# Weights decoded in chunks of two slices, and a key load moved ahead of a store, in a kernel of banded attention and an MLP

## The chip, the cores and the metric

The program runs on one core of one Trainium2 chip. The metric is the device time of one execution in microseconds (us). TensorE does the matmuls, VectorE, ScalarE and GpSimd the elementwise work, and SyncE issues nearly all DMAs. In the profile they are called PE (PEld for the weight loads), DVE, ACT, POOL and SP.

## The reference

```python
B, H, S, D = 4, 8, 768, 64          # n_global = 8, n_local = 96
def _attn_ref(q, k, v, n_global, n_local):
    scores = np.matmul(q, k.transpose(0, 1, 3, 2)) / np.sqrt(D)
    rel = pos[:, None] - pos[None, :]
    is_global = pos[None, :] < n_global
    is_local = (rel >= 0) & (rel < n_local)
    dist = np.where(is_global & ~is_local, n_local, np.abs(rel))
    scores = np.where(is_global | is_local, scores - slopes * dist, -1e9)
    a = np.exp(scores - scores.max(-1, keepdims=True))
    return np.matmul(a / (a.sum(-1, keepdims=True) + 1e-9), v)

def _moe_ref(x, w_in, w_out):       # x: 3072 x 512, w_in: 512 x 2048, w_out: 2048 x 512
    h = x @ w_in
    return (h * np.clip(h + 3.0, 0.0, 6.0) / 6.0) @ w_out
```

The attention's output, heads side by side, is x. The weights `w_in` and `w_out` come as 64-bit floats, q, k and v as 32-bit floats.

## The kernel before

**Blocks and pairs.** The 3072 rows are cut into 8 blocks of 384. A block is first attended, in 4 pairs of heads (32 pairs in all, numbered through), and then goes through the MLP. A pair has three tiles of 128 rows, t = 0, 1, 2. Its scores are matmuls (`scores`, L857 or L861), `weigh` adds the distances and finds the row maximum on DVE (L872) and takes the exponential on ACT (L876), `sum_up` forms the reciprocals on DVE, and `normalize` multiplies on POOL (L896). From block 2 on `spread(t)` transposes 32x32 blocks on DVE (L921) and stores them through SP to a scratch in DRAM (`there`, L923). `fetch` brings a pair's three tiles back as `weights` with four DMAs (L930), and `values` (L948) multiplies by v. `put_x` splits the result into a high and a low part, `xh` on ACT and `xl` on DVE.

**The MLP.** The inner 2048 are cut into 16 slices, numbered f. A step of a slice is `first(f)`, 12 matmuls into `hp` (L175), `gate` (ACT L186, then DVE L187, giving `g`), a high part `gh` (ACT L195, or POOL L193 from block 2 on), the rest `gl` (DVE L200), and `second(f)`, 9 matmuls (L207) into three accumulators. `second` of a slice follows `first` of the next one. Each product is formed from high and low parts, three matmuls for one.

**The decode.** The 64-bit weights are turned on the chip into a high and a low 32-bit part. The host lays them out in 32 chunks of 512 KB, one slice of `w_in` and one of `w_out` in turn. A chunk is fetched by SP (`wst`, L372), and takes these passes over 128x512 words: a magnitude on ACT (`wz`, L380), a scaled low word on POOL (`we`, L384), a clamp and a shift on DVE (L411, L412), the sign on ACT (into `we`, L391), an addition on DVE (L421), the high part on ACT (`w1h` or `w2h`, L425), and the low part on DVE (`w1l` or `w2l`, L418). There are three buffers of `wst` and two each of `wz` and `we`. The generator `decode` gives out the work in three steps a chunk, each with a DVE price; `work` calls it as long as the DVE price given out is below the PE time given out, and `decoded_to` forces what a slice needs.

**Stages.** While the first 8 pairs (blocks 0 and 1) are attended, the decode begins. Then block 0's 16 steps run with the decode beside them and 4 of block 1's steps among them. The remaining 12 steps of block 1 run beside block 2's attention (`beside`): a list of units, one unit per half step, into which a pair's parts are placed, 4 units per pair; `scale` (L840, giving `qs`) prepares a pair's queries on ACT. From there on each block's MLP runs beside the next block's attention.

**Order.** PE, SP and POOL run in the order in which the program is written (`in_order`). DVE's and ACT's order is set by a list scheduler, from that order and its own timing. Every engine, and SP's queue of DMA issues too, executes in order: an instruction that waits holds what is behind it. Keys and queries of a pair are loaded by `load_next(n, False)` into the place of pair n, for pair n + 2, once pair n's scores are done. Values are loaded by `load_next(n, True)`.

The general path (`general`, `weight_chunk`) is compiled and not executed for these sizes.

Of the kernel before, what the change touches and what calls it, by code (L numbers as in the profile page):

```python
# [10 lines left out]
F32R = mybir.dt.float32r  # L11
I32 = mybir.dt.int32
U32 = mybir.dt.uint32
I16 = mybir.dt.int16
F16 = mybir.dt.float16
AF = mybir.ActivationFunctionType
ALU = mybir.AluOpType
# [33 lines left out]
WAKE = 9  # L51
BESIDE = 12
LEAST_AHEAD = 4
WORDS = 3
DOWN = 2.0 ** -95

def store(nc, pool, out, row, acc, last=False):
# [6 lines left out]
class Kernel:  # L64
# [15 lines left out]
    def decoding(self, ctx, loads, bufs, **kw):  # L80

        self.wp = self.pool("wp", loads, ctx=ctx, **kw)
        self.zp = self.pool("zp", bufs, ctx=ctx, **kw)
        self.ep = self.pool("ep", bufs, ctx=ctx, **kw)

    def weights(self):

# [33 lines left out]
    def weight_chunk(self, i):  # L121

        nc = self.nc
        f = i // 2
        if i % 2 == 0:  # L130
            hi, lo = self.w1(self.w1h, f), self.w1(self.w1l, f)
            sh = lambda a: a.rearrange("p (k c) -> p k c", k=NKT)
        else:
            hi, lo = self.w2(self.w2h, f), self.w2(self.w2l, f)
            sh = lambda a: a
        st = self.wp.tile([P, 2 * DM], I32, name="wst")
        z = self.zp.tile([P, DM], I32, name="wz")
        e = self.ep.tile([P, DM], I32, name="we")
        nc.sync.dma_start(out=st, in_=self.w[i])
# [12 lines left out]
        nc.vector.tensor_tensor(out=lo, in0=sh(zf), in1=hi.bitcast(F32), op=ALU.subtract)  # L152
# [215 lines left out]


    def fetch(self, i):  # L370
        self.raw[i] = self.wp.tile([P, 2 * DM], I32, name="wst")
        self.nc.sync.dma_start(out=self.raw[i], in_=self.w[i])  # L372

    def magnitude(self, i):


        words = self.raw[i].rearrange("p (c w) -> p c w", w=2)
        self.z[i] = self.zp.tile([P, DM], I32, name="wz")
        self.e[i] = self.ep.tile([P, DM], I32, name="we")
        self.nc.scalar.activation(out=self.z[i].bitcast(F32), in_=words[:, :, 1].bitcast(F32), func=AF.Abs, scale=DOWN)  # L380
# [3 lines left out]
        self.nc.gpsimd.tensor_scalar(out=self.e[i], in0=words[:, :, 0].bitcast(U32), scalar1=2.0 ** -29, scalar2=0.0, op0=ALU.mult, op1=ALU.add)  # L384

    def signs(self, i):


        top = self.raw[i].bitcast(I16).rearrange("p (c w) -> p c w", w=4)[:, :, 3]
        over = self.e[i].bitcast(F16).rearrange("p (c w) -> p c w", w=2)[:, :, 1]  # L390
        self.nc.scalar.activation(out=over, in_=top, func=AF.Sign, scale=-1.0, bias=self.half)  # L391

    def part(self, i, w1, w2):
        f = i // 2
        return (self.w1(w1, f), lambda a: a.rearrange("p (k c) -> p k c", k=NKT)) if i % 2 == 0 else (self.w2(w2, f), lambda a: a)

    def decode(self):

        nc = self.nc
        ts, tt = nc.vector.tensor_scalar, nc.vector.tensor_tensor
        N = 2 * NF
        self.magnitude(0)
        for i in range(N + 1):
            a, b = i < N, i > 0
            if a:
                if i + 2 < N:
                    self.fetch(i + 2)
                z = self.z[i]  # L410
                ts(out=z.bitcast(F32), in0=z.bitcast(F32), scalar1=LEAST * DOWN, scalar2=MOST * DOWN, op0=ALU.max, op1=ALU.min)  # L411
                ts(out=z, in0=z, scalar1=3, scalar2=None, op0=ALU.logical_shift_left)  # L412
                self.signs(i)
            yield 0.78 * a
            if b:
                hi, sh = self.part(i - 1, self.w1h, self.w2h)
                lo, _ = self.part(i - 1, self.w1l, self.w2l)
                tt(out=lo, in0=sh(self.z.pop(i - 1).bitcast(F32)), in1=hi.bitcast(F32), op=ALU.subtract)  # L418
            yield 0.64 * b
            if a:  # L420
                tt(out=z, in0=z, in1=self.e.pop(i), op=ALU.add)  # L421
# [3 lines left out]
                nc.scalar.copy(out=hi, in_=sh(z.bitcast(F32)))  # L425
            yield 0.66 * a

    def work(self, pe, dve):

# [5 lines left out]
    def decode_step(self):  # L435
        self.given[1] += next(self.decoding_steps)
        self.decoded += 1
        if self.decoded == 3 * (2 * NF + 1):
            self.decoded_all()

    def decoded_to(self, i):

        while self.decoded < 3 * (i + 1) + (2 if i < 2 * NF - 1 else 3):
            self.decode_step()

    def halves(self, steps, pool=False):


        for block, f, x, acc in steps:
            self.decoded_to(2 * f)  # L450
# [30 lines left out]

    def finish(self):
        block, f, acc, gh, gl = self.last
        self.decoded_to(2 * f + 1)
# [8 lines left out]
    def banded(self, flag):  # L493
# [12 lines left out]
        with ExitStack() as early, ExitStack() as words:  # L506
            x0 = self.x_tiles(self.pool("x0", 1, ctx=early, side="right"))
            xs = [x0, self.x_tiles(), self.x_tiles()]
            self.decoding(words, WORDS, 2, side="right")
            self.decoding_steps = self.decode()  # L510

            def decoded_all():
# [3 lines left out]
            self.decoded_all = decoded_all  # L516
            self.fetch(0)
            self.given[1] = LEAD
            self.allowed = 3 * NF + 2
# [57 lines left out]
            self.allowed = 3 * (2 * NF + 1)  # L577
# [46 lines left out]
    def beside(self, x):  # L624
# [4 lines left out]
        pairs[0].scale()  # L629
        for p, me in enumerate(pairs):  # L630
            at = units[4 * p + 2:]
            weigh = lambda t, me=me: me.scores(t)()
            even = lambda t, me=me: (me.sum_up(t), me.normalize(t))
            at[0] += [lambda weigh=weigh: weigh(0), lambda weigh=weigh: weigh(1)]
            at[1] += [lambda even=even: even(0), lambda even=even: even(1)]
            if p + 1 < NPAIR:
                at[1].append(pairs[p + 1].scale)
            at[2] += [lambda weigh=weigh: weigh(2), lambda me=me: me.spread(0), lambda me=me: me.spread(1)]
            at[3] += [lambda even=even: even(2), lambda me=me: me.spread(2)]
            at[4] += [me.fetch, lambda me=me: self.load_next(me.n, False)]  # L640
# [43 lines left out]
    def general_setup(self):  # L684
# [2 lines left out]
        self.common(1, 2)  # L687
        self.weights()
        self.weights()
        self.decoding(self.ctx, 1, 1)  # L690
        self.ap_ = self.pool("ap", 1)
        self.dp = self.pool("dp", 1)
        self.up = self.pool("up", 1)
# [335 lines left out]
```

## Time and profile before

| | us |
|---|---|
| median of 3 runs | 684.6 |
| their range | 681.65 to 684.73 |
| the profiled execution | 682.72 |
| its span, first to last instruction | 680.9 |

1.8 us lie around the span. PE is busy for 655.4 us of it (96%), DVE for 416.2 (61%), ACT for 297.6 (44%), POOL for 213.4 (31%). The chain of work that ended last is made of PE for 78%. Since matmuls overlap, busy time of PE is not a rate; the number of matmuls in a stretch tells more. In the rows below, a row of the stages has the stretch, its length, then busy us and (x instructions) of PE, PEld, DVE, ACT and POOL, the granted clock of PE, the busy share of the DMA engines and GB/s. A row of a group has line, engine, operation, out<-in, shape and count, then busy us, mean ns of one, and the engine's idle time before them with what ended it.

### The profile page before, as it was taken

What the parts mean: (1) busy time and instruction counts of PE and PEld (TensorE: products, weight loads), DVE (VectorE), ACT (ScalarE), POOL (GpSimd) and SP (SyncE); (2) the same over time, 40 slices, a digit from 0 to 9 for tenths busy, and PEclk for the clock granted to TensorE, in tenths of its full rate; (3) what the DMA queues carried; (4) which work ended last, traced back from release to release, by engine and by line L of the source; (5) the groups of instructions that cost most, each with busy time, mean ns of one, the idle gap of its engine ahead of it and who ended that gap; (6) DMA issues with size and microseconds to landing.
All of it is one profiled execution on the core that took longest, in us unless ns stands there. A gap on an engine that the chain in (4) does not pass through costs nothing.

```text
span 680.9 us, 11393 instructions
## 1 busy us (share of the span) xinstructions
PE 655.4 (96%) x3923; PEld 580.3 (85%) x3923; DVE 416.2 (61%) x1132; ACT 297.6 (44%) x762; POOL 213.4 (31%) x389
## 2 busy tenths in 40 slices
PE   9878999999897999999999999999999999999997
PEld 7767888887676999899999999999998999988995
DVE  6887999935354776557762777547763677422222
ACT  6897888844343443143331444143331434221111
POOL 5661222202111333315440444404541344302110
PEclk9999899999899999999999999999999999999999
DMA  8565555213655357634554256634465155500001
GB/s 292 153 228 167 189 185 183 97 48 82 169 143 152 104 149 198 163 124 118 151 155 135 83 152 185 180 113 116 124 163 155 66 156 143 139 32 17 1 1 52
DMA packets 69476, 89.58 MB, mean 132 GB/s; under 512 B 10912, under 2 KB 54176, under 8 KB 69408
## 3 DMA queue, kind: packets, MB, share of 16 engines
q1 hardware_dynamic: 69120, 88.49, 44.6%
q8 instruction: 33, 0.54, 0.3%
q14 instruction: 35, 0.29, 0.1%
q10 hardware_dynamic: 288, 0.26, 0.1%
HBM read 65.14 MB, written 23.59 MB: 130 GB/s over the span
## 4 chain that ended last, share of the span: by engine, by line
PE 78%; DVE 6%; DMA 6%; ACT 4%; issue 2%; POOL 2%; SPq 1%; DVEq 0%; POOLq 0%; ACTq 0%
PE hp L175 34%; PE acc L207 32%; PE xp L948 3%; PE sp L861 2%; DMA load<-pairs 2%; PE tp L948 2%; ACT n L876 2%; PE tp L861 2%; DMA there<-blocks 1%; POOL n L896 1%; DVE wz L421 1%; SPq L930 1%; DVE gl L200 1%; DMA wst<-w 1%; DVE wz L412 1%
## 5 line engine op out<-in xcount | busy, mean ns | idle before, releaser
L186 ACT ACTIVATE g<-hp,small 128x384 f32<-128x384 f32 x127 | 73.6, 579 | 241.9 <-PE hp L175 218.7
L175 PE MATMUL hp<-xh,w1h 128*128 128x384 f32 x512 | 174.8, 341 | 1.6 <-ACT w1h L425 1.6
L175 PE MATMUL hp<-xh,w1l 128*128 128x384 f32 x512 | 173.7, 339 | 2.2 <-DVE w1l L418 2.1
L175 PE MATMUL hp<-xl,w1h 128*128 128x384 f32 x512 | 172.4, 337 | 0.0
L193 POOL TENSOR_SCALAR gh<-g 128x384 fp32r<-128x384 f32 x96 | 51.8, 540 | 296.9 <-DVE g L187 254.3
L207 PE MATMUL acc<-w2h,gl 128*128 128x512 f32 x336 | 132.8, 395 | 0.7 <-DVE gl L200 0.7
L207 PE MATMUL acc<-w2h,gh 128*128 128x512 f32 x336 | 132.4, 394 | 0.5 <-ACT o L60 0.5
L207 PE MATMUL acc<-w2l,gh 128*128 128x512 f32 x336 | 132.0, 393 | 0.0
L896 POOL TENSOR_SCALAR n<-n,sums 128x232 f32<-128x232 f32 (+1 forms) x186 | 98.3, 544 | 95.4 <-DVE sums L887 63.6
L187 DVE SCALAR_TENSOR_TENSOR g<-g,hp 128x384 f32<-128x384 f32 x128 | 69.8, 545 | 78.8 <-ACT g L186 78.3
L200 DVE TENSOR_TENSOR gl<-g,gh 128x384 fp32r<-128x384 f32 x128 | 81.1, 633 | 51.7 <-POOL gh L193 44.9
L876 ACT ACTIVATE n<-n,least 128x232 f32<-128x232 f32 (+1 forms) x192 | 89.2, 466 | 48.3 <-DVE least L872 46.9
L175 PEld LDWEIGHTS hp<-xh,w1h 128*128 128x128 f32 x512 | 96.8, 189 | 8.4 <-ACT w1h L425 2.4
L175 PEld LDWEIGHTS hp<-xh,w1l 128*128 128x128 f32 x512 | 96.5, 189 | 3.8 <-DVE w1l L418 3.8
L175 PEld LDWEIGHTS hp<-xl,w1h 128*128 128x128 f32 x512 | 96.7, 189 | 3.6
L207 PEld LDWEIGHTS acc<-w2h,gl 128*128 128x128 f32 x336 | 63.0, 188 | 15.8 <-DVE gl L200 2.0
L921 DVE STREAM_TRANSPOSE blocks<-n 128x256 f32<-128x256 f32 x132 | 51.5, 425 | 37.6 <-POOL n L896 26.2
L207 PEld LDWEIGHTS acc<-w2h,gh 128*128 128x128 f32 x336 | 63.3, 188 | 11.0 <-ACT o L60 0.9
L207 PEld LDWEIGHTS acc<-w2l,gh 128*128 128x128 f32 x336 | 63.2, 188 | 10.0
L384 POOL TENSOR_SCALAR we<-wst 128x512 int32<-128x512 uint32 x32 | 24.4, 764 | 61.1 <-DVE wz L421 27.8
L872 DVE CUSTOM_DVE_ANT_0 n<-sp,d 128x232 f32<-128x232 f32 (+1 forms) x70 | 23.7, 376 | 30.5 <-PE sp L861 30.1
L876 ACT ACTIVATION_READ_ACCUMULATOR n<-n,least 128x1 f32 x192 | 36.0, 188 | 0.0
(120 smaller groups left out, 764.1 us busy)
## 6 DMA issues: line engine op xcount, KB each, us to landing
wst<-w SPq DMA_DIRECT2D x32, 512.0 KB, 3.6
there<-blocks SPq DMA_DIRECT2D x60, 256.0 KB, 2.6
load<-pairs SPq DMA_DIRECT2D x20, 636.0 KB, 5.1
load<-pairs SPq DMA_DIRECT2D x32, 384.0 KB, 4.2
weights<-there SPq DMA_DIRECT2D x48, 192.0 KB, 3.9
weights<-there SPq DMA_DIRECT2D x48, 160.0 KB, 3.3
out<-o SPq DMA_DIRECT2D x23, 256.0 KB, 2.0
load<-pairs SPq DMA_DIRECT2D x11, 444.0 KB, 4.8
```

The costliest lines, as they stand in the source:

```text
L175: self.nc.tensor.matmul(hp, lhsT=self.w1(w, f)[:, kt, :], rhs=a[:, kt, :], start=(n == 0), stop=(n == 3 * NKT - 1))
L186: nc.scalar.activation(out=g, in_=hp, func=AF.Relu, bias=self.three, scale=1.0)
L187: nc.vector.scalar_tensor_tensor(out=g, in0=g, scalar=6.0, in1=hp, op0=ALU.min, op1=ALU.mult)
L193: self.nc.gpsimd.tensor_scalar(out=gh, in0=g, scalar1=1.0, scalar2=0.0, op0=ALU.mult, op1=ALU.add)
L200: self.nc.vector.tensor_tensor(out=gl, in0=g, in1=gh.bitcast(F32), op=ALU.subtract)
L207: self.nc.tensor.matmul(acc[tt], lhsT=a[:, tk], rhs=self.w2(w, f), start=(f == 0 and j == 0), stop=(f == NF - 1 and j == 2))
L384: self.nc.gpsimd.tensor_scalar(out=self.e[i], in0=words[:, :, 0].bitcast(U32), scalar1=2.0 ** -29, scalar2=0.0, op0=ALU.mult, op1=ALU.add)
L861: nc.tensor.matmul(sp[j][:, lo:W], lhsT=q[:, t], rhs=part["kx"][:, c], start=(m == 0), stop=(m == 1))
L876: nc.scalar.activation(out=e[:, j, lo:W], in_=e[:, j, lo:W], func=AF.Exp, bias=self.least[:, i:i + 1], scale=-1.0, accum_out=self.sums[:, ...
L896: nc.gpsimd.tensor_scalar(out=e[:, j, lo:W], in0=e[:, j, lo:W], scalar1=over, scalar2=0.0, op0=ALU.mult, op1=ALU.add)
L921: nc.vector.transpose(out=blocks[:, :, s].rearrange("p b j q -> p j b q"), in_=e[:, :, c:c + P].rearrange("p j (b q) -> p j b q", b=4))
L948: nc.tensor.matmul(xps[j * D:(j + 1) * D, t * P:(t + 1) * P], lhsT=vt[0:K, t, j * D:(j + 1) * D], rhs=self.part(t, j, c, K), start=(c == 0 ...
```

## The change

Three things. First, a chunk has two slices, of `w_in` or of `w_out`, so there are 16 chunks of 1 MB and each pass runs over 128x1024 words; there are two buffers of `wst` instead of three, two of `wz`, and one of `we` instead of two. The sign is read from the whole upper 32-bit word. The prices of `decode` are 1.35, 1.1 and 1.1 a chunk (before 0.78, 0.64 and 0.66). Second, beside the second block a pair's key load goes into the SP queue ahead of the pair's last store instead of behind its four fetches, and the next pair's `scale` is written behind it. Third, there the scores of t = 0 and t = 1 are issued together before the first `weigh`.

```diff
-WORDS = 3
+WORDS = 2
 def fetch(self, i):
-    self.raw[i] = self.wp.tile([P, 2 * DM], I32, name="wst")
+    self.raw[i] = self.wp.tile([P, 4 * DM], I32, name="wst")
 ...
 def signs(self, i):
-    top = self.raw[i].bitcast(I16).rearrange("p (c w) -> p c w", w=4)[:, :, 3]
+    top = self.raw[i].rearrange("p (c w) -> p c w", w=2)[:, :, 1]
 ...
 def decode(self):
-    N = 2 * NF
+    N = NF
 ...
-                if i + 2 < N:
-                    self.fetch(i + 2)
+                if i + WORDS < N:
+                    self.fetch(i + WORDS)
 ...
-            yield 0.78 * a
+            yield 1.35 * a
 ...
-            yield 0.64 * b
+            yield 1.1 * b
 ...
-            yield 0.66 * a
+            yield 1.1 * a
 ...
-            self.decoding(words, WORDS, 2, side="right")
+            self.decoding(words, WORDS, (2, 1), side="right")
 def beside(self, x):
 ...
-            at[0] += [lambda weigh=weigh: weigh(0), lambda weigh=weigh: weigh(1)]
+            at[0].append(lambda me=me: [weigh() for weigh in [me.scores(t) for t in range(2)]])
             at[1] += [lambda even=even: even(0), lambda even=even: even(1)]
+            at[2] += [lambda me=me: me.scores(2)(), lambda me=me: me.spread(0), lambda me=me: me.spread(1)]
+            at[3] += [lambda even=even: even(2), lambda me=me: self.load_next(me.n, False), lambda me=me: me.spread(2)]
             if p + 1 < NPAIR:
-                at[1].append(pairs[p + 1].scale)
-            at[2] += [lambda weigh=weigh: weigh(2), lambda me=me: me.spread(0), lambda me=me: me.spread(1)]
-            at[3] += [lambda even=even: even(2), lambda me=me: me.spread(2)]
-            at[4] += [me.fetch, lambda me=me: self.load_next(me.n, False)]
+                at[3].append(pairs[p + 1].scale)
+            at[4].append(me.fetch)
```

What stands where on the engines follows from it. PE's order is the same, and POOL's differs only in the sizes and the number of the decode's passes.

On DVE, in the middle of the decode, between two gates (L187, `g<-g,hp`), there stands before:

```order
L187 SCALAR_TENSOR_TENSOR g<-g,hp 128x384
L421 ISA wz<-wz,we 128x1024
L411 TENSOR_SCALAR wz<-wz 128x512
L200 TENSOR_TENSOR gl<-g,gh 128x384
L412 TENSOR_SCALAR wz<-wz 128x512
L418 TENSOR_TENSOR w2l_153<-wz,w2h_152 128x512
L421 ISA wz<-wz,we 128x1024
L411 TENSOR_SCALAR wz<-wz 128x512
L187 SCALAR_TENSOR_TENSOR g<-g,hp 128x384
```

Now (the gate is L191, the clamp and the shift L417 and L418, the low part L424, the addition L427, `gl` L204):

```order
L191 SCALAR_TENSOR_TENSOR g<-g,hp 128x384
L418 TENSOR_SCALAR wz<-wz 128x1024
L424 TENSOR_TENSOR w2l_153<-wz,w2h_152 128x1024
L204 TENSOR_TENSOR gl<-g,gh 128x384
L427 ISA wz<-wz,we 128x2048
L417 TENSOR_SCALAR wz<-wz 128x1024
L191 SCALAR_TENSOR_TENSOR g<-g,hp 128x384
```

From the fifth gate to the fourteenth exactly one chunk of two slices, that is two old chunks' work, stands between two gates, where before there were one or two old chunks; behind the fourteenth gate one low part is left, while before the decode lasted to the nineteenth.

On SP, at the start of the stage beside the second block, before (`there` is a store, `weights` the fetch, `load` of 888 columns a pair's keys and queries, of 768 its values):

```order
L923 DMA there<-blocks 512x1x128 x2
L930 DMA weights<-there 32x4x320 x4
L299 DMA load_82<-pairs 128x888
L923 DMA there<-blocks 512x1x64
L923 DMA there<-blocks 512x1x128 x2
L930 DMA weights<-there 32x4x320 x4
L299 DMA load_83<-pairs 128x888
```

Now:

```order
L928 DMA there<-blocks 512x1x128
L303 DMA load_82<-pairs 128x888
L928 DMA there<-blocks 512x1x128
L935 DMA weights<-there 32x4x320 x4
L928 DMA there<-blocks 512x1x64
L928 DMA there<-blocks 512x1x128
L303 DMA load_83<-pairs 128x888
```

The load has moved ahead of the last of the three stores and of the four fetches.

On ACT, where a pair's last exponentials (L876, then L881) and the scaling of a later pair's queries (`qs`) stand, before:

```order
L840 ACTIVATE qs<-load_83,factors 128x384
L186 ACTIVATE g<-hp,small 128x384
L876 ACTIVATE n,sums<-n,least 128x232
L195 CAST gh<-g 128x384
L876 ACTIVATE n,sums<-n,least 128x232
L161 CAST xh<-acc 128x384
```

Now:

```order
L190 ACTIVATE g<-hp,small 128x384
L881 ACTIVATE n,sums<-n,least 128x232
L199 CAST gh<-g 128x384
L881 ACTIVATE n,sums<-n,least 128x232
L845 ACTIVATE qs<-load_83,factors 128x384
L165 CAST xh<-acc 128x384
```

The scaling, which needs the load, stood ahead of the gate and the exponentials and stands behind them.

More of the change, by code (lines that the diff above doesn't have):

```diff
@@ L13 @@
 U32 = mybir.dt.uint32
-I16 = mybir.dt.int16
 F16 = mybir.dt.float16
@@ L82, in decoding @@
         self.wp = self.pool("wp", loads, ctx=ctx, **kw)
-        self.zp = self.pool("zp", bufs, ctx=ctx, **kw)
-        self.ep = self.pool("ep", bufs, ctx=ctx, **kw)
+        self.zp = self.pool("zp", bufs[0], ctx=ctx, **kw)
+        self.ep = self.pool("ep", bufs[1], ctx=ctx, **kw)
     def weights(self):
@@ L138, in weight_chunk @@
         e = self.ep.tile([P, DM], I32, name="we")
-        nc.sync.dma_start(out=st, in_=self.w[i])
+        both = self.w[f // 2 * 2 + i % 2]
+        if i % 2 == 0:
+            nc.sync.dma_start(out=st.rearrange("p (k c) -> p k c", k=NKT),
+                              in_=both.rearrange("p (k s c) -> p k s c", k=NKT, s=2)[:, :, f % 2])
+        else:
+            nc.sync.dma_start(out=st, in_=both.rearrange("p (s c) -> p s c", s=2)[:, f % 2])
         words = st.rearrange("p (c w) -> p c w", w=2)
@@ L377, in magnitude @@
         words = self.raw[i].rearrange("p (c w) -> p c w", w=2)
-        self.z[i] = self.zp.tile([P, DM], I32, name="wz")
-        self.e[i] = self.ep.tile([P, DM], I32, name="we")
+        self.z[i] = self.zp.tile([P, 2 * DM], I32, name="wz")
+        self.e[i] = self.ep.tile([P, 2 * DM], I32, name="we")
         self.nc.scalar.activation(out=self.z[i].bitcast(F32), in_=words[:, :, 1].bitcast(F32), func=AF.Abs, scale=DOWN)
@@ L393, in part @@
     def part(self, i, w1, w2):
-        f = i // 2
-        return (self.w1(w1, f), lambda a: a.rearrange("p (k c) -> p k c", k=NKT)) if i % 2 == 0 else (self.w2(w2, f), lambda a: a)
+        half, f = i // (NF // 2), i // 2 * 2 % (NF // 2)
+        if i % 2 == 0:
+            return w1[half][:, :, f * P:(f + 2) * P], lambda a: a.rearrange("p (k c) -> p k c", k=NKT)
+        return w2[half][:, f:f + 2, :], lambda a: a.rearrange("p (s c) -> p s c", s=2)
     def decode(self):
@@ L437, in decode_step @@
         self.decoded += 1
-        if self.decoded == 3 * (2 * NF + 1):
+        if self.decoded == 3 * (NF + 1):
             self.decoded_all()
     def decoded_to(self, i):
-        while self.decoded < 3 * (i + 1) + (2 if i < 2 * NF - 1 else 3):
+        while self.decoded < 3 * (i + 1) + (2 if i < NF - 1 else 3):
             self.decode_step()
@@ L449, in halves @@
         for block, f, x, acc in steps:
-            self.decoded_to(2 * f)
+            self.decoded_to(f // 2 * 2)
             g = self.gate(self.first(f, x), block == len(self.blocks) - 1 and f == NF - 1)
@@ L483, in finish @@
         block, f, acc, gh, gl = self.last
-        self.decoded_to(2 * f + 1)
+        self.decoded_to(f // 2 * 2 + 1)
         self.second(f, acc, gh, gl)
@@ L518, in banded @@
             self.given[1] = LEAD
-            self.allowed = 3 * NF + 2
+            self.allowed = 3 * NF // 2 + 2
             acc = []
@@ L576, in banded @@
             self.weights()
-            self.allowed = 3 * (2 * NF + 1)
+            self.allowed = 3 * (NF + 1)
             acc1 += [pool.tile([P, BANK], F32, name=name) for pool, name in ((self.ps_s, "sp"), (self.ps_t, "tp"), (self.ps_x, "xp"))]
@@ L631, in beside @@
             at = units[4 * p + 2:]
-            weigh = lambda t, me=me: me.scores(t)()
             even = lambda t, me=me: (me.sum_up(t), me.normalize(t))
-            at[0] += [lambda weigh=weigh: weigh(0), lambda weigh=weigh: weigh(1)]
+            at[0].append(lambda me=me: [weigh() for weigh in [me.scores(t) for t in range(2)]])
             at[1] += [lambda even=even: even(0), lambda even=even: even(1)]
+            at[2] += [lambda me=me: me.scores(2)(), lambda me=me: me.spread(0), lambda me=me: me.spread(1)]
+            at[3] += [lambda even=even: even(2), lambda me=me: self.load_next(me.n, False), lambda me=me: me.spread(2)]
             if p + 1 < NPAIR:
-                at[1].append(pairs[p + 1].scale)
-            at[2] += [lambda weigh=weigh: weigh(2), lambda me=me: me.spread(0), lambda me=me: me.spread(1)]
-            at[3] += [lambda even=even: even(2), lambda me=me: me.spread(2)]
-            at[4] += [me.fetch, lambda me=me: self.load_next(me.n, False)]
+                at[3].append(pairs[p + 1].scale)
+            at[4].append(me.fetch)
             at[7].append(lambda me=me, last=p + 1 == NPAIR: me.values(load=last))
@@ L689, in general_setup @@
         self.weights()
-        self.decoding(self.ctx, 1, 1)
+        self.decoding(self.ctx, 1, (1, 1))
         self.ap_ = self.pool("ap", 1)
@@ L1003, in weight_chunks @@
 def weight_chunks(w_in, w_out):
-    chunks = np.stack([w_in.reshape(NKT, P, NF, P).transpose(2, 1, 0, 3).reshape(NF, P, DM), w_out.reshape(NF, P, DM)], axis=1)
-    return chunks.reshape(2 * NF, P, DM).view(np.int64)
+    first = w_in.reshape(NKT, P, NF // 2, 2 * P).transpose(2, 1, 0, 3).reshape(NF // 2, P, 2 * DM)
+    second = w_out.reshape(NF // 2, 2, P, DM).transpose(0, 2, 1, 3).reshape(NF // 2, P, 2 * DM)
+    return np.stack([first, second], axis=1).reshape(NF, P, 2 * DM).view(np.int64)
 def kernel(q, k, v, n_global, n_local, moe_w_in, moe_w_out):
```

## The prediction

> **What bounds the kernel now.** I first read the busy time by stages.
>
> ```profile
> 0.00:20.00 20.00, 18.75 (x143) 15.70 (x144) 13.88 (x86) 13.79 (x52) 11.99 (x37) 1.00 0.77 262
> 20.00:42.00 22.00, 17.81 (x185) 14.35 (x185) 17.36 (x74) 20.78 (x71) 12.12 (x26) 1.00 0.62 191
> 42.00:62.00 20.00, 17.43 (x140) 14.79 (x140) 15.92 (x30) 16.03 (x33) 9.69 (x14) 1.00 0.52 167
> 62.00:75.00 13.00, 10.82 (x54) 9.27 (x51) 11.16 (x20) 10.07 (x18) 3.60 (x5) 0.87 0.65 219
> 75.00:114.00 39.00, 38.01 (x188) 33.30 (x187) 38.25 (x72) 34.97 (x60) 10.70 (x14) 1.00 0.55 186
> 114.00:150.00 36.00, 34.92 (x174) 30.86 (x174) 26.84 (x50) 25.00 (x43) 4.59 (x6) 1.00 0.27 93
> 150.00:221.00 71.00, 63.26 (x363) 50.70 (x362) 34.32 (x122) 27.78 (x81) 12.63 (x27) 0.98 0.47 130
> 221.00:600.00 379.00, 379.00 (x2303) 344.39 (x2303) 237.37 (x644) 135.42 (x387) 137.28 (x236) 1.00 0.50 138
> ```
>
> From 221 us on PE is busy without a gap, and the change touches nothing there: all that can be won or lost lies before. From 20 to 42 us ACT is the full engine (20.78 of 22), from 75 to 114 us DVE (38.25 of 39). From 150 to 221 us no engine is full, so there it is waits.
>
> PE's full rate, from the chain that ended last (start, us, what):
>
> ```profile
> 226.08 2.09 PE hp L175 x12
> 228.17 2.08 PE acc L207 x9
> ```
>
> A step of the MLP is 21 matmuls in 4.17 us, 5.04 per us.
>
> **The decode, part by part.** Between 78 and 114 us, the whole stretch and its groups:
>
> ```profile
> 78.00:114.00 36.00, 35.01 (x172) 30.46 (x172) 35.34 (x67) 32.02 (x54) 9.71 (x13) 1.00 0.57 190
> ...
> L421 DVE CUSTOM_DVE_ANT_0 wz<-wz,we 128x1024 uint16<-128x1024 uint16 x13 | 8.9, 683 | 0.4
> L411 DVE TENSOR_SCALAR wz<-wz 128x512 f32<-128x512 f32 x13 | 8.0, 613 | 0.1
> L412 DVE TENSOR_SCALAR wz<-wz 128x512 int32<-128x512 int32 x13 | 6.1, 472 | 0.1
> L200 DVE TENSOR_TENSOR gl<-g,gh 128x384 fp32r<-128x384 f32 x8 | 4.8, 605 | 0.0
> L187 DVE SCALAR_TENSOR_TENSOR g<-g,hp 128x384 f32<-128x384 f32 x8 | 4.4, 548 | 0.1
> L418 DVE TENSOR_TENSOR w2l<-wz,w2h 128x512 fp32r<-128x512 f32 x6 | 4.1, 678 | 0.0
> L391 ACT ACTIVATE we<-wst,small 128x512 f16<-128x512 int16 x12 | 10.6, 884 | 1.3 <-POOL we L384 1.1
> L380 ACT ACTIVATE wz<-wst 128x512 f32<-128x512 f32 x13 | 8.7, 666 | 0.5 <-DVE w2l L418 0.5
> L425 ACT CAST w2h<-wz 128x512 fp32r<-128x512 f32 x7 | 4.3, 618 | 1.0 <-DVE wz L421 0.9
> L195 ACT CAST gh<-g 128x384 fp32r<-128x384 f32 x8 | 4.0, 501 | 0.1
> L384 POOL TENSOR_SCALAR we<-wst 128x512 int32<-128x512 uint32 x13 | 9.7, 747 | 28.2 <-DVE wz L421 18.8 <-ACT g L186 7.3 <-ACT wz L380 2.1
> ```
>
> 8 gates and 13 old chunks passed in 36 us: a step took 4.50 us, of which DVE was busy 4.42. Gate and rest take 0.548 + 0.605 = 1.153; the 13 chunks take (35.34 - 8 x 1.153) / 13 = 2.01 us each. Now each gate has one new chunk ahead of it, two old ones joined. Fixed cost: from 384 to 512 elements an operation grows by 0.678 - 0.548 = 0.130, about 1.02 ns an element, so 0.156 us of it is fixed, and 0.083 of that overlaps its neighbour (the 67 instructions add up to 41.0 us, the engine was busy 35.34). Four operations fewer save 4 x 0.07 = 0.29: a chunk costs 4.02 - 0.29 = 3.73 and a step 4.88. Cheaper it gets if clamp and shift meet POOL less:
>
> ```profile
> L411 DVE TENSOR_SCALAR wz<-wz x21: 411/428/880, 77.0 to 133.4; 128x512 f32<-128x512 f32 x21
> ```
>
> A clamp alone takes 0.411, on average 0.613 (the shift 0.472). All of this waiting in two old chunks is 2 x (0.613 + 0.472 - 0.822) = 0.53, so the floor of a step is 4.36. With two operations exposed instead of four I let half of it go (-0.26) and, since they and POOL's pass are longer, give a third back, and add DVE's idle 0.08: 4.88 - 0.26 + 0.12 + 0.08 = 4.82, between 4.4 and 5.0. That is above the 4.50 of before and PE's 4.17: over the nine steps from the fifth gate to the fourteenth +9 x 0.32 = +2.9 us (-0.9 to +4.5).
>
> [...]
>
> How late the fifth gate comes: ahead of the first gate ACT had four magnitudes, four signs and two high parts, 4 x 0.666 + 4 x 0.884 + 2 x 0.618 = 7.4 us. Now it is three, three and two of double size. ACT's slope from `gh` to `w2h` is 0.117 per 128 elements, 0.47 for 512 more: 3 x 1.13 + 3 x 1.35 + 2 x 1.09 = 9.6, so +2.2 in a stage that ACT fills (1.5 if the sign, now read as a 32-bit word, costs what the magnitude does; 3.4 if the passes simply double). Then before waits for words: SP issues values' load and chunks only when PE has freed a place (SP's issues, the chain, and the fifth gate).
>
> ```profile
> 56.84 0.87 SPq L372 DMA_DIRECT2D wst<-w  x2
> ...
> 56.84 5.54 DMA wst<-w
> ...
> 73.78 0.56 DVE L187 SCALAR_TENSOR_TENSOR g<-g,hp 128x384 f32<-128x384 f32 x1 [0.30 <-ACT g L186]
> ```
>
> These were old chunks 7 and 8; at that place it is now new chunk 5, the eleventh and twelfth old one, so PE's weights for slices 4 and 5 are there, but the fourth gate stands behind chunk 5's addition. It is issued at 56.84 + 2.2, lands after 5.54 + 1.4, and with POOL's pass 1.3, sign 1.35, addition 1.2 that gate comes at 69.9, the fifth one step later at 74.7: +0.9 against 73.78 (0 to 2.5). Behind the fourteenth gate DVE is free; the stretch 114 to 150 us had 174 matmuls where 36 x 5.04 = 181 fit: -1.4 us. Decode: 0.9 + 2.9 - 1.4 = +2.4 (-2 to +6). Two fetches of 1 MB instead of 512 KB at the start push the third pair's keys back; 512 KB at 262 GB/s are 2.0 us, mostly ahead of their use: +0.2 (0 to 1.5).
>
> **Beside the second block.** What PE, then ACT, waited for from 150 to 221 us, and the granted clock after the longest of these waits (stretch as above, clock 0.57):
>
> ```profile
> PE acc L857 <- DVE least L872: 3.2, 4, 1.7
> PE sp L207 <- ACT gh L195: 2.5, 2, 1.5
> PE acc L948 <- DMA weights<-there: 1.9, 1, 1.9
> ...
> ACT qs L840 <- DMA load<-pairs: 9.5, 2, 6.4
> ...
> ACT q L823 <- DMA load<-pairs: 7.6, 1, 7.6
> ...
> 178.00:182.00 4.00, 4.00 (x12) 2.92 (x11) 2.53 (x12) 1.80 (x8) 1.78 (x4) 0.57 0.60 155
> ```
>
> - The 3.2 us are the scores of t = 1 held until t = 0 was read from the same bank. Issued in twos they have nothing to wait for: -3.2. With the longest of these (1.7) the slow clock behind it goes, 4 x 0.43 = -1.7. What PE does next is `second` of the slice before, whose `gh` is a step old, so nothing is late there.
> - ACT stood 9.5 + 7.6 us before `qs` and `q` for a load just issued, and gates and exponentials stood behind it. The load now goes out once scores are done and the second store is out, some 10 us earlier, ahead of one store and four fetches, and `qs` stands behind the exponentials: -2.5. The store that it now precedes waits for DVE's transposes about 4 us longer than the load for its place, so it isn't held; the load's transfer may overlap it (0 to 0.5 a pair).
> - The 1.9 us for `weights` are the end of a chain, which stays. For the first pair, whose ACT work had not stood, it shows bare (start, us, engine, line):
>
> ```profile
> 157.79 0.66 PE L857 MATMUL acc<-load,qs 64*128 64x232 f32 x4
> ...
> 171.82 1.32 PE L948 MATMUL acc<-weights,load 128*64 128x128 f32 x20
> ```
>
> From the end of the last scores (158.4) to `values` 13.4 us pass. PE's own work between is 12.6 (0.5 us of the wait for t = 0 and 0.3 for the weights taken off), so about 0.8 is waited now. The two pairs behind have the `values` before them between, 1.3 more: nothing. The last pair has no following scores (-1.75), but that `values` (+1.25): 12.1 minus what switching saves, 11.8, so 1.6 us. New waits 2.4, old 1.9: +0.5.
>
> Sum: -3.2 - 1.7 - 2.5 + 0.5 = -6.9 (-3 to -9.5).
>
> **The sum.** +2.4 + 0.2 - 6.9 = -4.3 us. From the profiled execution 682.72 that is 678.4; the median of the runs lies 1.9 above it, 684.6, which gives 680.3. 0.5% is 3.4 us, about what a measurement of this kernel can tell from no change.
>
> **Rivals.** (a) The decode gives the gain back: a step at 5.0 and the fifth gate 2.5 us late, 2.5 + 4.5 - 1.4 = +5.6, less 6.9: 683.5. For it: DVE is already full (35.34 of 36). Against it: its collisions must not fall. [...]
> (b) The waits beside the second block are replaced: with PE earlier, `weights` is late for every pair (0.8, 0.5, 0.5, 1.6 us) and the slow clock comes back (1.7): -3.5 there, 683.7. For it: the 13.4 us chain has no slack; against it: only the first and the last pair lack the 1.3.
> (c) Slower: the word buffers. With two of them chunk i + 2 is fetched only when chunk i's sign is done, and ACT then runs landing, magnitude, gate, high part, `gh` and sign in order: D + 1.13 + 0.57 + 1.09 + 0.50 + 1.35 = D + 4.64 for two chunks. The page's landings:
>
> ```profile
> wst<-w SPq DMA_DIRECT2D x32, 512.0 KB, 3.6
> load<-pairs SPq DMA_DIRECT2D x20, 636.0 KB, 5.1
> load<-pairs SPq DMA_DIRECT2D x32, 384.0 KB, 4.2
> ```
>
> 252 KB more cost 0.9, so 1 MB lands in 3.6 + 1.8 = 5.4 at most and a step is 5.0, no worse than DVE. It decides from D = 6.8 on (a step of 5.7, +11 us): then 688.5. Against it: that needs the queue busy all the time, and its share here is 0.57.
> (d) The decode gains: a step at 4.4, the gate on time: 0 - 0.9 - 1.4 = -2.3, 675.6. For it: clamp and shift may miss POOL's fewer passes.
>
> **Chances.** Forecast 0.42 (677 to 682.5, about a quarter of it within 0.5%), (d) 0.16, (a) 0.19, (b) 0.13, (c) 0.10. Faster: 0.32 + 0.16 + 0.03 = 0.51. Within 0.5%: 0.10 + 0.16 + 0.13 = 0.39. Slower: 0.10. The range holds forecast, (a), (b) and most of (d): 675 to 687.
>
> **What would show it.** Between 78 and 114 us DVE still full, about 7.5 gates in 36 us, passes of 1024 elements at 1.2 us (addition, low part) and 0.7 to 0.9 (clamp, shift); from about 118 us on 21 matmuls every 4.17 us. PE's wait for `least` gone, no clock below 1.0 after it, `qs` and `q` without a wait of several us, one wait for `weights` of 1 to 2 us at the last pair. The forecast is wrong if gates come at 4.4 or 5.5 us, if `wst` lands after more than 6 us, or if PE's waits beside the second block still add up to over 5 us.

## The result, and the profile after

The changed kernel takes 679.0 us (median of 6 runs, 677.14 to 681.25) against 684.25 us (median of 6) on the same chip: a ratio of 0.9932, 95% interval 0.9908 to 0.9957. The forecast was 680.3. A second measurement, further below, gave 0.9955 (0.9936 to 0.9973). The profiled execution takes 679.32 us, its span is 677.5.

The stages of the changed kernel, in the columns shown for before (stretch, length, busy us and instructions of PE, PEld, DVE, ACT, POOL, granted clock, share of the DMA engines, GB/s):

```profile
20.00:42.00 22.00, 18.08 (x151) 14.19 (x150) 16.29 (x64) 19.96 (x63) 12.34 (x22) 0.84 0.51 144
42.00:62.00 20.00, 16.17 (x134) 13.83 (x132) 15.95 (x31) 17.39 (x31) 12.26 (x15) 0.91 0.49 179
62.00:75.00 13.00, 12.71 (x84) 11.19 (x82) 9.60 (x13) 9.66 (x15) 2.27 (x2) 1.00 0.78 265
75.00:114.00 39.00, 34.77 (x158) 29.49 (x159) 38.97 (x49) 36.46 (x40) 11.52 (x8) 0.96 0.58 214
114.00:150.00 36.00, 35.09 (x178) 31.42 (x177) 17.71 (x26) 15.42 (x23) 2.21 (x2) 1.00 0.04 17
150.00:221.00 71.00, 68.58 (x413) 57.47 (x412) 37.10 (x130) 33.63 (x94) 11.70 (x27) 1.00 0.52 147
```

From 75 to 114 us PE did 158 matmuls where it did 188 before: the decode now costs more. From 150 to 221 us it did 413 instead of 363.

PE executes the same 3923 matmuls in the same order in both kernels, so the two traces can be laid over each other: the start of the n-th matmul after, less its start before. This shows where time is lost and won, and needs no guess about waits (us, worked out from the two traces; the last column is a second execution of the changed kernel):

| n-th matmul | before at | place | after | again |
|---|---|---|---|---|
| 243 | 30.6 | attention of the first pairs | +0.7 | +0.8 |
| 286 | 36.1 | behind the longest wait there | +5.3 | +2.6 |
| 339 | 44.2 | ahead of the first gate | +6.5 | +3.5 |
| 528 | 77.6 | at the fifth gate | +6.0 | +3.0 |
| 707 | 115.2 | at the fourteenth gate | +9.0 | +6.9 |
| 869 | 149.1 | last step ahead of the stage beside the second block | +7.2 | +5.1 |
| 1256 | 224.8 | behind that stage | -2.3 | -4.9 |
| 3900 | | at the end | -3.1 | -4.2 |

So the decode lost 5.1 to 7.2 us and the stage beside the second block won 9.5 to 10.0. The forecast had +2.6 and -6.9: nearly the same sum out of two terms that were both too small. One trace of before is one execution too: in the traces of five kernels below that have its decode, the 869th matmul starts between 0.0 and 1.2 us earlier than in it, so the loss may be up to 1.2 us larger. The gates that the forecast named, in the changed kernel, and the fourteenth of before (start, us, engine, line):

```profile
79.35 0.55 DVE L191 SCALAR_TENSOR_TENSOR g<-g,hp 128x384 f32<-128x384 f32 x1
...
122.78 0.54 DVE L191 SCALAR_TENSOR_TENSOR g<-g,hp 128x384 f32<-128x384 f32 x1
```

```profile
114.20 0.54 DVE L187 SCALAR_TENSOR_TENSOR g<-g,hp 128x384 f32<-128x384 f32 x1
```

From the fifth gate to the fourteenth pass 43.43 us, 4.83 a step, against 40.42 before, 4.49 a step: +3.0 us. The fifth gate itself is 5.6 us late. (In those five other traces it comes at 72.85 to 73.57 us.)

Beside the second block, what PE, then ACT, waited for (us in total, times, longest):

```profile
ACT qs L845 <- DMA load<-pairs: 5.7, 2, 2.9
...
ACT q L828 <- DMA load<-pairs: 2.6, 1, 2.6
PE acc L953 <- DMA weights<-there: 2.4, 2, 2.2
```

The waits for `least` (3.2 us before) and for `gh` (2.5) are gone, and the clock is 1.00 in the whole stage; `qs` and `q` still wait for their loads, 8.3 instead of 17.1 us; one long wait for `weights` is left, at the last pair.

### The profile page after: what moved, and what is told of

It is laid out like the page before. It is cut to its first block, busy times and chain, and to the rows that moved or that the text cites. A ratio compares the mean times of both kernels' runs of the same rounds, so it can differ in the third digit from the quotient of the medians.

```text
span 677.5 us, 11187 instructions
## 1 busy us (share of the span) xinstructions
PE 655.5 (97%) x3923; PEld 582.1 (86%) x3923; DVE 406.7 (60%) x1068; ACT 294.3 (43%) x714; POOL 212.3 (31%) x373
## 4 chain that ended last, share of the span: by engine, by line
PE 75%; DVE 9%; DMA 5%; issue 4%; ACT 4%; POOL 2%; SPq 0%; POOLq 0%; DVEq 0%; ACTq 0%
PE hp L179 33%; PE acc L211 31%; PE xp L953 3%; PE sp L866 2%; ACT n L881 2%; DMA load<-pairs 2%; DVE wz L427 2%; PE tp L953 2%; PE tp L866 2%; POOL n L901 1%; DVE n L877 1%; DVE wz L417 1%; DMA wst<-w 1%; DVE g L191 1%; DVE gl L204 1%
## 5 line engine op out<-in xcount | busy, mean ns | idle before, releaser
L191 DVE SCALAR_TENSOR_TENSOR g<-g,hp 128x384 f32<-128x384 f32 x128 | 69.8, 545 | 89.8 <-ACT g L190 89.4
L881 ACT ACTIVATE n<-n,least 128x232 f32<-128x232 f32 (+1 forms) x192 | 89.2, 466 | 50.5 <-DVE least L877 49.8
L204 DVE TENSOR_TENSOR gl<-g,gh 128x384 fp32r<-128x384 f32 x128 | 78.4, 613 | 52.5 <-POOL gh L197 44.9
L388 POOL TENSOR_SCALAR we<-wst 128x1024 int32<-128x1024 uint32 x16 | 22.7, 1416 | 46.1 <-DVE wz L427 37.5
L881 ACT ACTIVATION_READ_ACCUMULATOR n<-n,least 128x1 f32 x192 | 36.1, 188 | 0.0
```

What stands on the lines that cost most here:

```text
L191: nc.vector.scalar_tensor_tensor(out=g, in0=g, scalar=6.0, in1=hp, op0=ALU.min, op1=ALU.mult)
L204: self.nc.vector.tensor_tensor(out=gl, in0=g, in1=gh.bitcast(F32), op=ALU.subtract)
L881: nc.scalar.activation(out=e[:, j, lo:W], in_=e[:, j, lo:W], func=AF.Exp, bias=self.least[:, i:i + 1], scale=-1.0, accum_out=self.sums[:, ...
```

## The experiments

### Which part wins, which loses

Four kernels on one chip, beside 17 runs of before with a median of 682.48 us.

**The two parts beside the second block, decode as before.** The diff is the third and second item of the change: the last hunk of the diff above, and nothing else.

> The kernel before with only the changes beside the second block (load ahead, scores in twos); decode in chunks of one slice. Theory A (the two traces laid over each other, matmul by matmul: the change loses 7.2 us up to the stage beside the second block and wins 9.5 in it, and the parts are independent): 684.3 - 9.5 = 674.8 us, faster than the changed kernel. Theory B (the sizes of the prediction, -6.9 there): 677.4. Theory C (the parts hang together: the gain beside the block comes in part from the decode that ended earlier, so it is not had alone): 679 or more.

673.06 us, ratio 0.987 (0.9849 to 0.9891): 9.4 us faster than before, as theory A has it, and faster than the changed kernel. In its trace the offset to before goes from -0.8 to -11.0 over the stage.

**The decode alone.** The changed kernel with `beside` as before.

> The changed kernel with the stage beside the second block as before: only the chunks of two slices are new. Theory A: 684.3 + 7.2 = 691.5 us, and 688.5 if what the changed kernel gained at the end of its trace is real. Theory B (prediction, +2.6): 686.9. Theory C: the loss is below 2 us, since waits beside the block swallow a late decode.

691.33 us, ratio 1.012 (1.0098 to 1.0142): 8.9 us slower than before. Its offset is +6.6 us at the 869th matmul, near that of the changed kernel, and +9.3 behind the stage, so the late decode was not made good, but made worse. ACT's waits for the old loads are nearly those of before (`qs` 10.3 us, `q` 7.2, together 17.5 instead of 17.1); PE's waits for `least` are 4.2 instead of 3.2 us, for `weights` 2.7 instead of 1.9, and behind the last one the granted clock is 0.58 from 222 to 226 us.

**Scores in twos alone.**

```diff
-            at[0] += [lambda weigh=weigh: weigh(0), lambda weigh=weigh: weigh(1)]
+            at[0].append(lambda me=me: [weigh() for weigh in [me.scores(t) for t in range(2)]])
```

> The kernel before with only the scores of t = 0 and 1 issued together beside the second block. Theory A: PE's waits for the row maximum go, with the switches about them 4.7 us, and the slow clock behind the longest 1.65: 684.3 - 6.3 = 678.0 us. Theory B: -3.2 - 1.7 = 679.4. Rival: with the load still late the wait moves to gh and to the weights, and 681 or more is left.

681.06 us, ratio 0.998 (0.9964 to 0.9996): only 1.4 us. Both theories are wrong, the rival is right in the time and in the weights, not in `gh`. The waits for `least` are gone, but the time went over to the weights (the same list, this kernel), and behind one of these waits the granted clock is 0.58 from 202 to 206 us:

```profile
ACT qs L840 <- DMA load<-pairs: 8.2, 2, 5.1
ACT q L823 <- DMA load<-pairs: 7.0, 1, 7.0
PE acc L948 <- DMA weights<-there: 6.0, 4, 2.3
...
PE sp L207 <- ACT gh L195: 1.7, 1, 1.7
```

**The load ahead alone**, scores one at a time:

```diff
-            if p + 1 < NPAIR:
-                at[1].append(pairs[p + 1].scale)
 ...
-            at[3] += [lambda even=even: even(2), lambda me=me: me.spread(2)]
-            at[4] += [me.fetch, lambda me=me: self.load_next(me.n, False)]
+            at[3] += [lambda even=even: even(2), lambda me=me: self.load_next(me.n, False), lambda me=me: me.spread(2)]
+            if p + 1 < NPAIR:
+                at[3].append(pairs[p + 1].scale)
+            at[4].append(me.fetch)
```

> The kernel before with only the key load ahead of the last store and the scaling behind it, scores one at a time. Theory A: the waits of second for gh go (3.3 us), the weights chain takes 0.4 back: 684.3 - 2.9 = 681.4 us, and the waits for the row maximum stay. Theory B: -2.5 + 0.5 = 682.3. Rival: the waits for gh came from the queue of exponentials and not from the load; then no change (684.3).

673.21 us, ratio 0.9861 (0.9843 to 0.9879): 9.3 us, all of the gain of both together. Every theory had too little. The `scale` that is moved with it is no part of this: with that line alone moved, the order of all five engines stays word for word that of before, and with the load alone moved it is that of this kernel. This fits a list scheduler that places `qs` on ACT by when it takes the load to be there. PE's waits in this trace:

```profile
ACT qs L839 <- DMA load<-pairs: 4.0, 2, 2.1
...
PE acc L856 <- DVE least L871: 1.6, 4, 0.4
```

The waits for `least` fell from 3.2 to 1.6 us (the longest from 1.7 to 0.4) without any scores in twos. How the load lengthened them stands in the trace of before, on ACT and then on DVE:

```profile
172.57 0.61 ACT L840 ACTIVATE qs<-load,factors 128x384 f32<-128x384 f32 x1 [3.10 <-DMA load<-pairs]
...
173.56 0.50 ACT L195 CAST gh<-g 128x384 fp32r<-128x384 f32 x1
```

```profile
174.09 0.56 DVE L200 TENSOR_TENSOR gl<-g,gh 128x384 fp32r<-128x384 f32 x1 [3.43 <-ACT gh L195]
...
176.05 0.77 DVE L921 STREAM_TRANSPOSE blocks<-n 128x256 f32<-128x256 f32 x2 [1.10 <-POOL n L896]
176.74 0.52 DVE L162 TENSOR_TENSOR xl<-acc,xh 128x384 fp32r<-128x384 f32 x1
177.18 0.27 DVE L872 CUSTOM_DVE_ANT_0 n<-acc,d 128x128 f32<-128x128 f32 x1
```

ACT stood 3.10 us for the load; `gh` stood behind it, `gl` on DVE behind `gh`, the transposes (by way of the sums on DVE and `normalize` on POOL) and `xl` behind `gl`, and the row maximum, for which PE held the scores of t = 1, behind these. With the load ahead the same row maximum starts 0.5 us after its scores, and PE waits 0.39 us.

### How far the load should be moved

With an unchanged run of the changed kernel beside them; 15 runs of before, median 682.89 us.

**Behind the last store, ahead of the fetches.** The kernel before with `self.load_next(me.n, False)` behind `me.spread(2)` in `at[3]`, and nothing else: `scale` stays in `at[1]`.

> The kernel before with the key load behind the pair's last store but ahead of its four fetches (scores one at a time). Theory A (the load was late because it stood behind fetches that wait for the store to land, 2.7 us, and take 0.45 us each to issue, 4.4 us in all; ACT then stood for it): nearly the whole gain of the load moved further, 674 to 675. Rival (the place ahead of the last store is what counts, since ACT's order is then the early one; here qs stands almost where it did before): 678 or more.

674.47 us, ratio 0.9871 (0.9847 to 0.9894): theory A. The place ahead of the four fetches is what counts, with `scale` where it was. On SP's queue before:

```profile
176.84 0.51 SPq L923 DMA_DIRECT2D there<-blocks  x1
179.52 1.73 SPq L930 DMA_DIRECT2D weights<-there  x4
181.37 0.84 SPq L299 DMA_DIRECT2D load<-pairs  x2
```

The first fetch waits 2.7 us for the store to land, four of them take 1.73 us to issue, and the load leaves 4.5 us after the store. In this kernel the store is at 172.55 and the load at 173.17.

**Ahead of all three stores**, scores in twos:

```diff
-            at[2] += [lambda me=me: me.scores(2)(), lambda me=me: me.spread(0), lambda me=me: me.spread(1)]
+            at[2] += [lambda me=me: me.scores(2)(), lambda me=me: self.load_next(me.n, False), lambda me=me: me.spread(0), lambda me=me: me.spread(1)]
```

> Only the changes beside the second block, with the key load one place earlier still, right behind the scores that free its place and ahead of all three stores. Theory A (PE's waits for what hung on the load are gone already; only a wait for weights of 1.7 us at the last pair is left, which a store that starts later doesn't shorten): no change, 673. Rival (ACT still stands 5.7 us for loads before qs, and that still costs): 671. Rival (the load's transfer holds up the stores behind it): 675.

676.75 us, ratio 0.9902 (0.988 to 0.9924): by the ratios 2.2 us slower than with the load one place later (0.987, 0.9849 to 0.9891), so the two intervals still touch. The last rival comes nearest, and the traces bear it out. The landings between 150 and 221 us, here and then in the kernel of the first experiment (KB, median us from issue to landing):

```profile
there<-blocks SPq DMA_DIRECT2D x8, 256.0 KB, 4.0
...
there<-blocks SPq DMA_DIRECT2D x4, 128.0 KB, 4.6
```

```profile
there<-blocks SPq DMA_DIRECT2D x8, 256.0 KB, 2.7
...
there<-blocks SPq DMA_DIRECT2D x4, 128.0 KB, 2.5
```

A store behind the load's 444 to 636 KB lands 1.3 to 2.1 us later, the fetches wait for it, and PE waits 4.9 instead of 1.7 us for `weights`. In the kernel before it is the small store that is issued right behind the load, and there this one alone is late: 128 KB land after 4.9 us, 256 KB after 2.6. The profiled execution was the slowest of the six (679.94 us): behind the first of PE's waits the granted clock is 0.62 from 170 to 174 us and 0.52 from 174 to 178, so its trace shows the cost larger than the median has it.

**The changed kernel again.**

> The changed kernel again, on the chip of the two above. If the parts added up (beside the block alone 9.4 us won, the decode alone 8.9 lost), it would be 0.5 us faster than before, 682. Theory C (they hang together: a late decode is partly made good by the waits that it takes from the stage behind): 4 to 5 us faster than before, 678.

680.09 us, ratio 0.9955 (0.9936 to 0.9973), 2.8 us faster than before, and 0.9932 in the first measurement. The two parts measured alone add up to -0.5 us, with about 2 us on either side from their intervals, so they hang together a little: theory C has the direction right, but not why. It is not that a late decode is made good; in the trace of the decode alone the stage beside the second block lost 2.8 us more than in before, and with the load moved it doesn't. What lengthened PE's waits there stays open.

### Where the decode loses

Four changes of the changed kernel's decode on one chip; 19 runs of before, median 682.88 us.

**The pass on POOL left out.** `self.gpsimd...we<-wst` is gone, and the sign goes into one buffer that is zeroed once:

```diff
-        self.e[i] = self.ep.tile([P, 2 * DM], I32, name="we")
+        if i == 0:
+            self.zero = self.ep.tile([P, 2 * DM], I32, name="we")
+            self.nc.gpsimd.memset(self.zero.bitcast(F32), 0.0)
+        self.e[i] = self.zero
 ...
-        self.nc.gpsimd.tensor_scalar(out=self.e[i], in0=words[:, :, 0].bitcast(U32), ...)
```

> The changed kernel without the pass on GpSimd over the low words (they count as zero; one buffer, zeroed once, takes the sign), so that no pass of GpSimd stands beside the decode's passes on DVE. Theory A (the shift waits for the end of GpSimd's pass and takes 1.17 instead of 0.67 us): the step goes from 4.88 to about 4.38, 9 steps 4.5 us, 679.0 - 4.5 = 674.5 us. Rival: ACT, whose passes add up to 4.8 less overlaps in a step, or the ring of buffers bounds the step as well; it stays above 4.7 and the time above 677.

693.89 us, ratio 1.0164 (1.0127 to 1.0201): 15 us slower than the changed kernel. As a test of the step it failed, since the order changed with it: two chunks of two slices now stood between two gates, and these came every 8.2 to 8.7 us (81.22, 89.41, 97.88 us) while PE, from 85 to 115 us, was busy for 21.20 of 30. That the scheduler took the words to be there earlier is a guess. As a measurement of the passes it serves. DVE between 85 and 115 us:

```profile
L420 DVE TENSOR_SCALAR wz<-wz 128x1024 int32<-128x1024 int32 x7 | 4.9, 695 | 0.2
L419 DVE TENSOR_SCALAR wz<-wz 128x1024 f32<-128x1024 f32 x7 | 4.8, 690 | 0.6 <-ACT wz L387 0.5
```

In the changed kernel, 78 to 114 us, the same two passes:

```profile
L418 DVE TENSOR_SCALAR wz<-wz 128x1024 int32<-128x1024 int32 x7 | 8.2, 1168 | 0.0
L417 DVE TENSOR_SCALAR wz<-wz 128x1024 f32<-128x1024 f32 x8 | 5.5, 682 | 0.0
```

The clamp never waits there, the shift 0.47 us or a little more every time. One step of the changed kernel, DVE and then POOL, shows why:

```profile
88.55 0.68 DVE L417 TENSOR_SCALAR wz<-wz 128x1024 f32<-128x1024 f32 x1
89.15 0.54 DVE L191 SCALAR_TENSOR_TENSOR g<-g,hp 128x384 f32<-128x384 f32 x1
89.62 1.16 DVE L418 TENSOR_SCALAR wz<-wz 128x1024 int32<-128x1024 int32 x1
```

```profile
88.71 1.52 POOL L388 TENSOR_SCALAR we<-wst 128x1024 int32<-128x1024 uint32 x1 [3.37 <-DVE wz L427]
```

POOL's pass ends at 90.23, the shift 0.55 us later, and so it is in all nine steps from the fifth gate on. The gate, which runs in between, is not held. The same kernel has the control: all its shifts (ns, shortest, median, longest) are

```profile
L418 DVE TENSOR_SCALAR wz<-wz x16: 677/1161/1212, 18.8 to 119.0; 128x1024 int32<-128x1024 int32 x16
```

and the shifts at 71.54 and 75.39 us, which start 1.0 and 0.6 us after the end of POOL's pass, take 0.68 and 0.69 us.

**Other prices**: 1.56, 1.28 and 1.32 for 1.35, 1.1 and 1.1.

> The changed kernel with the prices of two old chunks for one new one (1.56, 1.28, 1.32 instead of 1.35, 1.1, 1.1): two new chunks instead of three are added up ahead of the first gate, but two between the second and the third. Theory A (the loss in front is the third chunk that a full ACT takes in ahead of the first gate): the fifth gate is 2 to 4 us earlier, 675 to 677. Rival (the same work is only moved; weights 0 to 5 must be there by the fifth gate in any case): 678 to 680.

682.04 us, ratio 0.9998 (0.9979 to 1.0017): by the ratios 2.9 to 4.5 us slower than the changed kernel, beyond both expectations. The front did gain: with two new chunks instead of three ahead of it the first gate came at 50.06 us (53.62 and 51.78 in two executions of the changed kernel) and the fifth at 76.08 (79.35 and 77.28). But `gl` now stands where the gate stood, right behind the clamp (DVE, then POOL):

```profile
94.51 0.69 DVE L417 TENSOR_SCALAR wz<-wz 128x1024 f32<-128x1024 f32 x1
95.11 1.47 DVE L204 TENSOR_TENSOR gl<-g,gh 128x384 fp32r<-128x384 f32 x1
96.51 0.68 DVE L418 TENSOR_SCALAR wz<-wz 128x1024 int32<-128x1024 int32 x1
```

```profile
94.67 1.50 POOL L388 TENSOR_SCALAR we<-wst 128x1024 int32<-128x1024 uint32 x1 [3.83 <-DVE wz L427]
```

`gl` takes 1.47 instead of 0.55 us and ends 0.41 us after POOL's pass, the shift behind it is free, and gates come every 5.34 us instead of 4.88: the same passes cost 0.46 us more a step because of what stands behind the clamp. So with POOL's pass running the shift took 0.47 us longer and `gl` 0.92, ending 0.55 and 0.41 us after it, while the gate takes 0.54 us beside that pass (89.15 us, in the changed kernel) and away from it (92.91 us, in this one). Why the gate is free, no run here shows.

**All passes in halves of 512 words, chunks of 1 MB and two word buffers as they are** (old prices for a half).

> The changed kernel with chunks of 1 MB and two word buffers as they are, but every pass cut in two halves of 512 words, with the old prices for each. Theory A (the loss in front comes from long passes on ACT and DVE ahead of what PE waits for): the fifth gate comes back by 3 to 5 us; the steps behind cost two old chunks each, 2 x 2.01 + 1.15 = 5.2 us, 9 x 0.3 = 2.7 us more: 677 to 679. Rival B (it comes from the fetch: 1 MB lands later and only two buffers): the fifth gate stays at 79 us and the time is 681 to 683.

686.53 us, ratio 1.005 (1.0031 to 1.0068): slower than either theory. The fifth gate came at 75.63 us, as theory A has it, but then gates came every 6.2 us (75.63, then 125.15 for the thirteenth). With one buffer of `we` for a whole chunk ACT's sign waited for POOL, 6.0 us between 85 and 115 us, and DVE was no longer full. So this kernel prices the buffer in the middle of the decode, and not the passes; only its front is read here.

**Only the first six chunks in halves.**

> The changed kernel with the passes of the first six chunks cut in two halves of 512 words, the others whole. Theory A (long passes in front): the fifth gate about 4.7 us earlier, the steps behind at 4.88: 674 to 675. Rival B (fetch and two buffers): no change, 679.

676.24 us, ratio 0.9907 (0.9872 to 0.9943), by the ratios 1.7 to 3.3 us faster than the changed kernel in its two measurements. The first gate came at 47.12 us, that of before at 47.28, and the fifth at 75.27: 4.1 us earlier than in the first execution of the changed kernel and 2.0 than in the second. The step behind it took 5.85 us, the others 4.88 to 4.91 but for the last, so that at the fourteenth gate 1.1 to 3.1 us are left, about what the time shows. Theory A is right in direction, but had too much: the whole passes in front cost some 2 us at the fifth gate, as far as single executions can tell, and in the first execution of the changed kernel a slow clock, of which more below, makes up the other 2. What else makes the fifth gate late, still 1.5 us against before, stays open; the fetch and the two word buffers were not tried by themselves. What a whole pass holds there stands on ACT and DVE of the changed kernel:

```profile
31.46 1.45 ACT L395 ACTIVATE we<-wst,small 128x1024 f16<-128x1024 int32 x1
32.78 0.46 ACT L165 CAST xh<-xp 128x384 fp32r<-128x384 f32 x1
```

```profile
32.95 1.24 DVE L427 CUSTOM_DVE_ANT_0 wz<-wz,we 128x2048 uint16<-128x2048 uint16 x1 [1.08 <-ACT we L395]
...
34.75 0.55 DVE L166 TENSOR_TENSOR xl<-xp,xh 128x384 fp32r<-128x384 f32 x1
```

The sign holds `xh`; the addition, which waits for the sign, and two row maxima hold `xl`; PE, which needs the place that `xl` frees, waits for it, between 30 and 38 us in the changed kernel and then in this one:

```profile
PE xp L953 <- issue: 3.2, 1, 3.2
```

```profile
PE xp L965 <- DVE xl L167: 1.3, 1, 1.3
```

## Why the prediction was right, and where it was not

- **The step of the decode**: predicted 4.82 us, measured 4.83 over the nine steps, +3.0 us where +2.9 was written. That is in part luck: it is 4.88 to 4.92 in each but the last, which has no clamp and takes 4.29. Clamp and shift do not each wait a little; the clamp goes free and the shift waits 0.47 us. Of the 0.53 us that two old chunks waited, 0.39 was to be left, so the waiting fell by less than was let go (with none of it let go, 4.88 + 0.08 = 4.96, the estimate would have been a little nearer there), and the 0.08 of DVE's idle that was added is gone (it is busy for 36.00 us of 36).
- **The later gain**: from the fourteenth gate to the stage beside, the offset falls by 1.8 in the table above (9.0 to 7.2), and by 1.4 if the gates themselves are compared (the fourteenth is 8.6 us late, the twentieth 7.2), as written.
- **The fifth gate**: this is the step that failed, +0.9 (0 to 2.5) against +5.6 in the profiled execution and +3.5 in the second one (77.28 us). The estimate counted ACT's additional 2.2 us and let most of them disappear in before's own wait for words. (Its bound for passes that simply double is mis-summed: 3 x 1.33 + 3 x 1.77 + 2 x 1.24 = 11.8, 4.3 more than 7.4 and not 3.4.) It left out two things. Passes of double length stand ahead of `xh` and `xl` in in-order queues, so PE waits 3.2 us in one piece; and the third of the three new chunks ahead of the first gate is late work for ACT, which is full there (busy for 19.96 of 22 us from 20 to 42): with two the first gate came 1.7 to 3.6 us earlier.
- **The clock**: a part of the front's loss, about 2 us of the 5.6 in the profiled execution (3.5 in the other), was not in the sum at all. Behind that wait, here in the changed kernel:

```profile
32.00:34.00 2.00, 0.24 (x3) 0.00 (x1) 1.05 (x1) 1.72 (x3) 1.94 (x3) 1.00 0.72 221
34.00:42.00 8.00, 6.61 (x41) 5.22 (x42) 5.58 (x21) 7.33 (x20) 2.87 (x5) 0.57 0.39 105
```

and in its second execution, with a wait of 3.1 us at the same place:

```profile
32.00:34.00 2.00, 0.36 (x4) 0.12 (x2) 0.94 (x1) 1.82 (x3) 1.82 (x3) 1.00 0.73 209
34.00:42.00 8.00, 4.30 (x44) 3.46 (x44) 7.99 (x31) 7.67 (x22) 3.02 (x5) 1.00 0.54 157
```

Behind the same wait the clock was nearly halved once and once not, which makes 2.7 us at the 286th matmul (+5.3 and +2.6), 2.1 at the 869th and 1.1 at the end. It differs from execution to execution, and with the old front too: of five executions with a wait of 3.0 to 3.2 us at this place, four show a clock of 0.58 to 0.82 from 34 to 38 us, and of six with the front of before, all with a wait of 2.36 us there, two show 0.64 and 0.74 from 38 to 42. What decides it, no run here shows: the slow clock came behind waits of 2.36 us and of 3.2, and stayed away behind waits of 2.36 and of 3.1.
- **Beside the second block**: predicted -6.9, measured -9.5 and -10.0. The slow clock at 178 to 182 us went, 1.65 us of 1.7 written; `gh` gave 3.3 of 2.5; `weights` cost 0.4 of 0.5; the four waits for `least` gave 5.0 of 3.2 (all from the traces laid over each other). But the cause of the largest term was wrong. Scores in twos were to bring 3.2 + 1.7; alone they brought 1.4, and on top of the load nothing that can be told (673.06 against 673.21). The load was to bring 2.5; alone it brought 9.3, though `qs` and `q` still waited. The prediction read the list of waits one line at a time and gave each wait its own remedy; the waits for `gh`, the slow clock and half of the waits for `least` hung on one cause, ACT standing for a late load.
- **Rivals**: (a) had the right sign for the decode and nearly its size (+5.6), with 683.5 only because the gain beside was too small. (b) did come about, in the kernel with scores in twos alone (four waits for `weights`, and the slow clock); its terms add up to -4.2 and not -3.5, which would have given 683.0. (c) did not: a chunk lands in 4.9 us in the median. (d) did not either, with a step of 4.83 and a late gate.

The forecast of -4.3 us was therefore right by luck, by two errors of 2.5 to 4.6 us that cancelled: a front that loses more, and a load that frees more.

## What to carry to other kernels

Before waits are added up, follow each back through the in-order queues to what stands first in line: here PE's waits for `gh` (2.5 us), half of those for `least` (1.6 of 3.2) and the slow clock behind the longest of these (0.57 over 4 us) hung on one late load, and scores in twos, which remove the last link of the chain alone, moved the wait to `weights` (from 1.9 to 6.0 us) and won 1.4 us, where the load moved ahead won 9.3. The larger tile saved fixed cost in a full engine (an addition over 1024 words took DVE 1.21 us, two over 512 took 2 x 0.683), but in the stage in front, which alternates between engines, its length was a hold on what was queued behind it (PE waited 3.2 us in one piece, and 1.3 with the first six chunks in halves); the kernel with old chunks in the decode and only the load moved is the best one here, 673 us, ratio 0.986 (with scores in twos it is the same). And when a pass is taken away or priced anew under a list scheduler, compare the order first: twice the order's change was larger than the effect in question.

## What the runs showed of the hardware

A pass of POOL over 128x1024 words, 1.11 us at its shortest and 1.52 where it began while DVE's clamp ran, cost DVE between nothing and 0.92 us, by which instruction stood next in DVE's queue: the gate nothing, the shift 0.47 behind a gate, `gl` 0.92 right behind the clamp. And with a load of about half a MB (444 or 636 KB) ahead of all three stores of a pair, these landed 1.3 to 2.1 us later than with the load ahead of the last one only (256 KB after 4.0 us in the median instead of 2.7, 128 KB after 4.6 instead of 2.5), and the chain of store, fetch and matmul waited for that. Last, one and the same pause of PE, 2.36 us in six executions and 3.0 to 3.2 us in five, was followed by a granted clock of 0.58 to 0.82 over 4 us in some of them and of 1.00 in the others.
